# Moving two pieces of matmul work in the head of a gated linear-attention and MLP kernel

## The chip, the cores and the metric

The kernel runs on one core of one Trainium2 chip. The metric is the device time of one execution in microseconds (us). Each kernel also has the profile of one execution. For the kernel before it is a further one; for every later kernel it is the first of the six timed ones, and the other five leave no trace. Its span is about 1.3 us shorter than the device time of that same execution (146.8 against 148.1 us before the change). An execution is marked slow when it is over 1.5% above the fastest of the same kernel, and fast otherwise; only fast ones are compared. The granted clock, the share of TensorE's full clock that the profile reports, was 1.0 in all fast executions.

## The reference, cut to what matters

The kernel computes `g * A(x) + (1 - g) * B(x)` for 2048 tokens of 512 features in bf16. `B` is a two-layer MLP with ReLU (512 to 1376 to 512). `A` is linear attention with 32 heads of 16, whose q and k logits go through a small per-head matrix `w_phi` and a softmax.

```python
pq = einsum("bhsd,hdf->bhsf", q, w_phi);  pk = einsum("bhsd,hdf->bhsf", k, w_phi)
phi_q = concat([softmax(pq), softmax(-pq)]);  phi_k = concat([softmax(pk), softmax(-pk)])
kv = einsum("bhsf,bhsd->bhfd", phi_k, v)          # ... o = (phi_q kv) / den;  a = o @ wo
h  = maximum(x @ w1, 0);  b = h @ w2
return g * a + (1 - g) * b
```

## The kernel before: the parts that the change touches

The kernel is hand-scheduled: each engine has a fixed list of operations, and named events become semaphore waits. TensorE (PE) begins with dummy matmuls, transposes the first 512 tokens of x (`x0`) in three pieces, and then computes the first eight 128-wide units of the MLP's hidden layer for these tokens. Each unit has a PSUM bank of its own, and all eight banks are in use. A "slab" is one 128-row block `t` of W1 applied to the eight units; four slabs add up to the hidden layer. The third piece of x0 (its last quarter, 128 tokens) is transposed into bank 1, the bank that unit 7 needs as well.

```python
# ... loads on SyncE's queue, in this order: x0 pieces 0 and 1, then
loadw1(0, 0, 4 * P, "a")          # W1 row block 0, units 0..3
loadx0(2)                         # last quarter of x0
loadw1(0, 4 * P, 8 * P)           # W1 row block 0, units 4..7
for t in range(1, NDT):
    loadw1(t, 0, 8 * P)           # W1 row blocks 1, 2, 3: 256 KB each
# ... rest of W1, w_phi, WV, then the q and the k weights (transposing loads), then x chunks 1..3

UB = (3, 4, 5, 0, 6, 7, 2, 1)     # bank of each unit
def slab(t, us=range(8), c0=0, c1=512):
    for u in us:                  # one matmul; columns c0:c1 are tokens
        p.op("pe", ... W1[:, t, u*P:(u+1)*P], XT[:, t, c0:c1] ...,
             after=["w10a" if t == 0 and u < 4 else f"w1{t}"]
                   + (free[UB[u]] if c0 == 0 else []) + [XV[h][t] for h in hs], ...)

slab(0, range(4), 0, 384)
for dt in range(4):
    xtr(2, dt, 1, dt * P)         # transpose the last x0 quarter into bank 1
xev("dve", 2, 0, 4, 1)            # VectorE empties bank 1 into XT
slab(0, range(4, 8), 0, 384)      # unit 7 waits for that copy
slab(0, range(8), 384, 512)
for t in range(1, NDT):
    slab(t)
# ... ReLUs, two more units, v tiles 0 and 1
for i in range(4): pre(i)         # q weights times w_phi -> copies pc0..pc3
vtile(2, "dve")
for i in range(4, 8): pre(i)      # k weights times w_phi -> copies pc4..pc7; pc4, pc6 on VectorE
rest(0)                           # 16 small matmuls
# main loop: atile(0) is first
def atile(m):                     # q logits into bank 0, k logits into bank 1
    first = xready(m // 4) + ([f"pc{i}" for i in range(8)] if m == 0 else [])
    order = [(dt, w) for dt in range(NDT) for w in range(2)]    # q and k in turn
    ...
```

The softmax here doesn't subtract the row's maximum and nothing guards it: scores larger than these inputs give would overflow.

## Time and profile before

| | before |
|---|---|
| device time, the three runs at hand before the prediction | 147.78, 147.81, 148.31 us |
| span of the profiled run | 146.8 us |
| TensorE busy | 142.6 us, 97% |
| first slab matmul / first matmul after the four slabs / first atile matmul | 4.73 / 12.36 / 19.59 us |

These lines are from the page of the kernel before: TensorE's busy time, the row of the granted clock in 40 slices, and the chain of work that ended last, by engine.

```profile
PE 142.6 (97%) x969; PEld 73.6 (50%) x986; DVE 92.5 (63%) x157; ACT 72.6 (49%) x125; POOL 52.2 (36%) x62
...
PEclk9999999999999999999999999999999999999999
...
PE 93%; DMA 2%; DVE 2%; issue 1%
```

TensorE is the bound. Next is the view of waits for TensorE: who waited for whom, total us, times, longest.

```profile
PE PS L235 <- DVE ONE L211: 0.4, 1, 0.4
PE PS L332 <- DVE WQK L317: 0.4, 1, 0.4
PE PS L524 <- DVE VS L554: 0.3, 1, 0.3
PE PS L524 <- DMA W<-in_B_w_dram: 0.2, 1, 0.2
```

There are four waits, all in the first 20 us. The change goes for the second and third lines. Next is TensorE's timeline around the first slab (start, duration, what, and in brackets the idle time before it and its releaser).

```profile
3.52 0.95 PE L241 MATMUL PS<-IDN,OT 128*128 128x128 bf16 x7
4.73 0.82 PE L524 MATMUL PS<-XT,W 128*128 128x384 bf16 x4 [0.25 <-DMA W<-in_B_w_dram]
5.39 0.39 PE L241 MATMUL PS<-IDN,OT 128*128 128x128 bf16 x4
5.61 0.65 PE L524 MATMUL PS<-XT,W 128*128 128x384 bf16 x3
6.56 1.00 PE L524 MATMUL PS<-XT,W 128*128 128x384 bf16 x10 [0.30 <-DVE VS L554]
```

The three 384-column matmuls that start at 5.61 us are units 4 to 6; unit 7 comes at 6.56 us. L554 in the bracket is a memset that follows the copy on VectorE: the copy itself is the first of the next lines, which are VectorE's, the second being the two k-weight copies.

```profile
5.81 0.69 DVE L253 CAST XT<-PS 128x512 bf16<-128x512 f32 x1 [1.60 <-PE PS L241]
...
18.33 1.21 DVE L317 CAST WQK<-PS 128x480 bf16<-128x480 f32 x2
```

The x0 copy ends at 6.50 us and unit 7 starts 0.06 us later. The second k-weight copy ends at 19.54 us, and the first atile matmul starts at 19.59 us, as TensorE's timeline there shows:

```profile
18.36 0.86 PE L290 MATMUL PS<-W,XT 128*128 128x97 bf16 x16
19.59 1.59 PE L332 MATMUL PS<-WQK,XT 128*128 128x480 bf16 x7 [0.38 <-DVE WQK L317]
```

The bracket understates such a hole: the profile only models where a matmul ends, and it draws one of 384 columns about 0.33 us long where the next can start 0.163 us after it. The distance between the starts of two matmuls that follow each other without a wait is called a slot here (0.163 us for 384 columns, 0.043 us for the 97 columns of the rest matmuls). The start-to-start loss is the distance between two starts less the slot of the first. The first hole is 6.562 - 5.937 - 0.163 = 0.46 us, and the second 19.595 - 19.008 - 0.043 = 0.54 us. All "losses" below are start-to-start.

The last line of this section is the DMA of W1's second row block, issued at 2.42 us: size, and us from issue to landing.

```profile
W<-in_B_w_dram SPq DMA_DIRECT2D x1, 256.0 KB, 3.7
```

### The profile page before, as it was taken

What the parts mean: (1) busy time and instruction counts of PE and PEld (TensorE: products, weight loads), DVE (VectorE), ACT (ScalarE), POOL (GpSimd) and SP (SyncE); (2) the same over time, 40 slices, a digit from 0 to 9 for tenths busy, and PEclk for the clock granted to TensorE, in tenths of its full rate; (3) what the DMA queues carried; (4) which work ended last, traced back from release to release, by engine and by line L of the source; (5) the groups of instructions that cost most, each with busy time, mean ns of one, the idle gap of its engine ahead of it and who ended that gap; (6) DMA issues with size and microseconds to landing.
All of it is one profiled execution on the core that took longest, in us unless ns stands there. A gap on an engine that the chain in (4) does not pass through costs nothing.

```text
span 146.8 us, 2536 instructions
## 1 busy us (share of the span) xinstructions
PE 142.6 (97%) x969; PEld 73.6 (50%) x986; DVE 92.5 (63%) x157; ACT 72.6 (49%) x125; POOL 52.2 (36%) x62
## 2 busy tenths in 40 slices
PE   8899989999999999999999999999999999999994
PEld 4544654444545544645645555554444444444443
DVE  3427736777688778678698976675444555555342
ACT  3307457887778778877878863022222111111150
POOL 2040001788768678787869820300000000000000
PEclk9999999999999999999999999999999999999999
DMA  5999992038349966335533430454433322322213
GB/s 163 319 266 230 166 234 52 0 71 76 71 80 311 177 196 94 71 71 107 78 71 71 107 71 20 91 108 111 83 82 82 75 71 70 78 71 74 71 43 107
DMA packets 45349, 16.12 MB, mean 110 GB/s; under 512 B 39352, under 2 KB 44824, under 8 KB 45336
## 3 DMA queue, kind: packets, MB, share of 16 engines
q1 hardware_dynamic: 45184, 15.92, 50.0%
q8 instruction: 8, 0.13, 0.4%
q10 hardware_dynamic: 152, 0.03, 0.1%
q14 instruction: 5, 0.04, 0.1%
HBM read 4.41 MB, written 2.10 MB: 44 GB/s over the span
## 4 chain that ended last, share of the span: by engine, by line
PE 93%; DMA 2%; DVE 2%; issue 1%
PE PS L486 25%; PE PS L278 19%; PE PS L332 18%; PE PS L495 9%; PE PS L407 9%; PE PS L524 5%; PE PS L461 3%; PE PS L429 3%; DMA W<-in_B_w_dram 2%; PE PS L290 1%; DVE WQK L509 1%; PE PS L312 1%; DVE XT L253 0%; DVE VS L415 0%; DVE WQK L317 0%
## 5 line engine op out<-in xcount | busy, mean ns | idle before, releaser
L486 PE MATMUL PS<-W,HT 128*128 128x512 bf16 (+3 forms) x182 | 40.2, 366 | 0.3
L375 POOL TENSOR_TENSOR EB<-EB,SC 128x1024 bf16<-128x1024 bf16 x15 | 28.9, 1930 | 25.0 <-DVE SC L373 25.0
L351 ACT ACTIVATE EB<-PS 128x480 bf16<-128x480 f32 (+1 forms) x44 | 30.1, 756 | 14.8 <-PE PS L332 14.8
L500 ACT ACTIVATE TFA<-PS,GT 128x512 bf16<-128x512 f32 x16 | 11.0, 687 | 42.7 <-PE PS L495 36.6
L278 PE MATMUL PS<-XT,W 128*128 128x512 bf16 x124 | 30.2, 379 | 0.2
L332 PE MATMUL PS<-WQK,XT 128*128 128x480 bf16 x128 | 28.5, 366 | 0.4 <-DVE WQK L317 0.4
L371 DVE TENSOR_REDUCE ZB<-EB 128x64 f32<-128x1024 bf16 x15 | 18.3, 1220 | 14.8 <-ACT EB L351 14.8
L509 DVE SCALAR_TENSOR_TENSOR WQK<-PS,OMG,TFA 128x512 bf16<-128x512 f32 (+2 forms) x17 | 12.2, 719 | 23.6 <-ACT TFA L500 22.4
L486 PEld LDWEIGHTS PS<-W,HT 128*128 128x128 bf16 (+1 forms) x187 | 17.0, 98 | 17.4
L264 ACT ACTIVATE HT<-PS 128x512 bf16<-128x512 f32 x35 | 20.3, 614 | 7.7 <-PE PS L524 5.9
L332 PEld LDWEIGHTS PS<-WQK,XT 128*128 128x128 bf16 x128 | 12.5, 98 | 14.1 <-DVE WQK L317 0.5
L278 PEld LDWEIGHTS PS<-XT,W 128*128 128x128 bf16 x128 | 12.0, 98 | 13.2
L386 DVE TENSOR_REDUCE ZB<-EB 128x64 f32<-128x1024 bf16 x16 | 18.6, 1164 | 0.0
L395 POOL TENSOR_TENSOR EB<-EB,SC 128x512 bf16<-128x512 bf16 x16 | 16.9, 1059 | 1.3
L495 PE MATMUL PS<-WO,OT 128*128 128x512 bf16 x62 | 16.0, 378 | 0.1
L407 PE MATMUL PS<-WV,XT 128*128 128x512 bf16 x59 | 15.3, 378 | 0.3
L471 DVE TENSOR_TENSOR WQK<-PS,RDEN 128x512 bf16<-128x512 f32 x16 | 11.1, 692 | 0.6
L495 PEld LDWEIGHTS PS<-WO,OT 128*128 128x128 bf16 x64 | 6.1, 97 | 7.2
L417 ACT ACTIVATE VS<-PS 128x512 bf16<-128x512 f32 x14 | 8.5, 608 | 2.0 <-PE PS L407 2.0
L373 DVE RECIPROCAL SC<-ZB 128x64 f32<-128x64 f32 x16 | 8.8, 553 | 0.5
L407 PEld LDWEIGHTS PS<-WV,XT 128*128 128x128 bf16 x64 | 5.5, 97 | 4.9
L524 PE MATMUL PS<-XT,W 128*128 128x512 bf16 (+2 forms) x39 | 7.4, 336 | 0.6 <-DVE VS L554 0.3
(57 smaller groups left out, 87.5 us busy)
## 6 DMA issues: line engine op xcount, KB each, us to landing
out_dram<-WQK SPq DMA_DIRECT2D x15, 128.0 KB, 1.7
W<-in_B_w_dram SPq DMA_DIRECT2D x2, 640.0 KB, 5.3
W<-in_B_w_dram SPq DMA_DIRECT2D x3, 256.0 KB, 3.9
WV<-in_A_wqkv_dram SPq DMA_DIRECT2D x1, 512.0 KB, 5.8
WO<-in_A_wo_dram SPq DMA_DIRECT2D x2, 256.0 KB, 3.2
W<-in_B_w_dram SPq DMA_DIRECT2D x1, 352.0 KB, 5.3
OT<-in_A_x_dram SPq DMA_DIRECT2D x1, 256.0 KB, 2.8
OT<-in_A_x_dram SPq DMA_DIRECT2D x2, 128.0 KB, 3.1
```

The costliest lines, as they stand in the source:

```text
L264: p.op("act", lambda e: e.activation(dst, src, ACT.Relu), after=[f"h{c}_{kt}"], ev=ev)
L278: p.op("pe", lambda e, t=t: e.matmul(PS[:, bank, :], W1[:, t, kt * P:(kt + 1) * P], XT[:, t, c * 512:(c + 1) * 512], start=(t == 0), stop= ...
L332: p.op("pe", lambda e, dt=dt, which=which: e.matmul(PS[:, which, 0:DE], XT[:, dt, m * P:(m + 1) * P], WQK[:, which, dt * DE:(dt + 1) * DE] ...
L351: p.op("act", lambda e: e.activation(dst, s_, ACT.Exp, scale=scale), after=[f"qk{m}"] + busy, ev=ev)
L371: p.op("dve", lambda e: e.tensor_reduce(zk, ek, AX.X, ALU.add), after=[emk, f"cst{b}"], ev=f"zk{m}")
L375: p.op("pool" if m < NT - 1 else "dve", lambda e: e.tensor_tensor(EB[:, b, 3, :].rearrange("p (g f) -> p g f", f=DH), EB[:, b, 2, :].rearr ...
L386: p.op("dve", lambda e: e.tensor_reduce(ZB[:, b, 0:64].rearrange("p (h s) -> p h s", s=2), bass.AP(tensor=EB, offset=base, ap=[[EBS, P], [ ...
L395: p.op("pool", lambda e: e.tensor_tensor(EB[:, b, 0, :].rearrange("p (h s f) -> p h s f", h=H, s=2)[:, :, 1, :], EB[:, b, 1, :].rearrange( ...
L407: p.op("pe", lambda e, dt=dt: e.matmul(PS[:, bank, :], XT[:, dt, m * P:(m + 1) * P], WV[:, dt, :], start=(dt == 0), stop=(dt == NDT - 1)), ...
L486: p.op("pe", lambda e, kt=kt, M=M: e.matmul(PS[:, bank, 0:n], HT[0:M, kt, m * P:(m + 1) * P], W2[0:M, kt, cs], start=(kt == 0), stop=(kt = ...
L495: p.op("pe", lambda e, t=t: e.matmul(PS[:, bank, :], OT[:, t, m * P:(m + 1) * P], WO[:, t, :], start=(t == 0), stop=(t == NDT - 1)), after ...
L524: p.op("pe", lambda e, u=u: e.matmul(PS[:, UB[u], c0:c1], W1[:, t, u * P:(u + 1) * P], XT[:, t, c0:c1], start=(t == 0 and c0 == 0), stop=( ...
```

## The change

The intent is to give TensorE something to do in both holes. Three units of the second slab are begun while the last x0 quarter is still being emptied, and atile 0 runs its four q matmuls first, which need only the first half of the weight copies.

```diff
 def atile(m):
-            first = xready(m // 4) + ([f"pc{i}" for i in range(8)] if m == 0 else [])
+            first = xready(m // 4)
             ...
+            if m == 0:
+                order = [(dt, w) for w in (0, 1) for dt in range(NDT)]
             ...
-                    after=(first if i == 0 else []) + (free[which] if dt == 0 else []),
+                    after=(first if i == 0 else []) + (free[which] if dt == 0 else [])
+                    + ([f"pc{4 * which + c}" for c in range(4)] if m == 0 and dt == 0 else []),
 # in slab():
-                    ... + (free[UB[u]] if c0 == 0 else [])
+                    ... + (free[UB[u]] if c0 == 0 and t == 0 else [])
 # order of the head:
-        slab(0, range(4, 8), 0, 384)
+        slab(0, range(4, 7), 0, 384)
+        slab(1, range(3), 0, 384)
+        slab(0, (7,), 0, 384)
         slab(0, range(8), 384, 512)
+        slab(1, range(3), 384, 512)
+        slab(1, range(3, 8))
 ...
-        for t in range(1, NDT):
+        for t in range(2, NDT):
             slab(t)
```

Below, "the slab half" is the new order of the head, and "q-first" is the atile half.

More of the change, by code (lines that the diff above doesn't have):

```diff
@@ L526, in slab @@
                     start=(t == 0 and c0 == 0), stop=(t == NDT - 1), skip_group_check=True),
-                    after=["w10a" if t == 0 and u < 4 else f"w1{t}"] + (free[UB[u]] if c0 == 0 else [])
+                    after=["w10a" if t == 0 and u < 4 else f"w1{t}"] + (free[UB[u]] if c0 == 0 and t == 0 else [])
                     + [XV[h][t] for h in hs],
```

## The prediction

> What bounds the kernel. The page gives TensorE 142.6 of 146.8 us (97%), and the chain of work that ended last is 93% TensorE matmuls; the granted clock is full throughout. The table of waits for TensorE shows only four idle stretches, all in the first 20 us: 0.4 us at the very start, 0.25 us for the first piece of W1, 0.30 us in the first slab, 0.38 us ahead of the first atile. No other engine holds TensorE up later. The change goes for the last two stretches. Nothing is removed; only the order changes, so those two holes are the ceiling.
>
> Their true size is from start to start, because the modelled end of a matmul includes its drain. The Trainium skill, "TensorE: Matmul & The Clock Gate", section "Wait — 56ns, not 53.3ns?", gives N / 2.4 GHz + 2.5 ns back to back when warm; the trace agrees (512 columns every 216 ns, 384 every 163, 128 every 56).
> - Hole 1: the last 384-column matmul before it starts at 5.94 us, the next at 6.56 us: 0.625 us for a slot of 0.163, so 0.46 us lost. Unit 7 uses bank 1, which VectorE empties of the last x0 quarter from 5.81 to 6.50 us.
> - Hole 2: the last gate/rest matmul starts at 19.01 us, the first atile matmul at 19.59 us: 0.587 for a slot of 0.043, so 0.54 us lost. It waits for the last of VectorE's two q/k weight copies, pc4 (18.33 to 18.97) and pc6 (18.89 to 19.54).
>
> What the change does.
> (a) Three 384-column matmuls of the second slab (3 x 0.163 = 0.49 us) go into hole 1. They need the second W1 row block. In the trace that DMA is issued at 2.42 us and lands at about 6.15 us (3.7 us from issue to landing), while TensorE would get there at 6.10 us. So I expect a small new wait on that DMA, about 0.1 us, and then no wait for VectorE: the three end their slots at about 6.68 us, after 6.50. Gain 0.36 us (0.1 to 0.46 with the landing).
> (b) With q first, atile 0 needs pc0 to pc3 (done by 17.5) and bank 0, which pc4 frees at 18.97; the rest matmuls end their slots at 19.05, so no wait. Four q matmuls of 0.203 us keep TensorE busy until 19.86 (on the old clock), and pc6 is done at 19.54 us. Hole 2 closes fully: 0.54 us. The 0.36 us shift of (a) moves the copies too, since they follow TensorE, so the two add.
>
> How much stays. Everything later follows TensorE. The x chunks land from 19.07 us and are first used at 22.3; the second q/k weight block lands at 15.43 and is used at 17.5: room for 0.9 us. I expect the sum, 0.90 us, to reach the end.
>
> Predicted time: 147.81 - 0.90 = 146.9 us; 8 times in 10 between 146.5 and 147.4 us (runs before spread over 0.5 us). Chances: faster by over 2% 0.01, within 2% 0.98, slower 0.01.
>
> What would show it: in the waits for TensorE, the VectorE entry of 0.30 us in the slab and of 0.38 us before the atile are gone; instead perhaps one below 0.1 us on the W1 DMA near 6.1 us, at the first second-slab matmul. In the timeline the first atile matmul follows the rest matmuls at one slot's distance, near 18.7 us, and later stages all come 0.9 us earlier.
>
> What would make it wrong: the second W1 block landing later than 6.6 us (then (a) gives nothing); a new wait between the q and k halves on ScalarE's copies (pc5, pc7, done at 19.17); an evacuation or transfer later that was just in time and now holds TensorE; or run-to-run spread as large as the gain.

## The result, and the profile after

| | before | after |
|---|---|---|
| device time, median of 6 runs | 148.05 (147.78 to 148.46) us | 147.51 (147.33 to 147.78) us |
| ratio of fast runs, 95% interval | | 0.9963, 0.9941 to 0.9986 |
| span of the profiled run | 146.8 us | 146.4 us |
| first slab / after the four slabs / first atile | 4.73 / 12.36 / 19.59 us | 4.35 / 12.51 / 19.20 us |

A ratio is the mean time of one kernel's fast runs over the mean of the other's in the same rounds, so it is not quite the ratio of the medians quoted.

The time, 147.51 us, lies 0.11 us above the predicted range, and the gain was 0.54 us where 0.90 us was forecast. Here are the same views of the changed kernel. The page:

```profile
PE 142.3 (97%) x972; PEld 73.2 (50%) x989; DVE 92.4 (63%) x157; ACT 72.5 (50%) x125; POOL 52.1 (36%) x62
...
PEclk9999999999999999999999999999999999999999
...
PE 93%; DMA 3%; SPq 1%; issue 1%; DVE 1%
```

The waits of TensorE:

```profile
PE PS L527 <- DMA W<-in_B_w_dram: 0.8, 3, 0.5
PE PS L235 <- DVE ONE L211: 0.4, 1, 0.4
```

Both VectorE waits of the table before are gone. In their place the wait for pieces of W1 has grown from one of 0.2 us to three with 0.8 us in total. The timeline around the first slab:

```profile
3.83 0.34 PE L241 MATMUL PS<-IDN,OT 128*128 128x128 bf16 x3
4.35 0.82 PE L527 MATMUL PS<-XT,W 128*128 128x384 bf16 x4 [0.19 <-DMA W<-in_B_w_dram]
5.01 0.39 PE L241 MATMUL PS<-IDN,OT 128*128 128x128 bf16 x4
5.56 0.66 PE L527 MATMUL PS<-XT,W 128*128 128x384 bf16 x3 [0.16 <-DMA W<-in_B_w_dram]
6.71 0.82 PE L527 MATMUL PS<-XT,W 128*128 128x384 bf16 x4 [0.48 <-DMA W<-in_B_w_dram]
```

The last line begins with the first second-slab matmul, at 6.71 us. The matmul before it starts at 5.893 us, so 6.705 - 5.893 - 0.163 = 0.65 us are lost, more than the 0.46 us of the hole that was to be filled. Its releaser is the DMA of W1's second row block. Another 0.32 us were lost just before, ahead of unit 4 (5.56 us): the second piece of W1's first row block landed at 5.51 us here, against 5.43 us before, while the matmuls came earlier. That wait is not of the new order, since unit 4 stands at the same place in the old one; but there it would have come out of VectorE's hole, as the trace of r_q_first below shows (0.07 us lost on this piece, then 0.38 us on VectorE).

This is the transfer of the second row block, issued at 2.42 us as before; it now took 4.2 us to land, at 6.66 us instead of 6.15:

```profile
W<-in_B_w_dram SPq DMA_DIRECT2D x1, 256.0 KB, 4.2
```

And TensorE around the first atile:

```profile
18.51 0.86 PE L290 MATMUL PS<-W,XT 128*128 128x97 bf16 x16
19.20 1.78 PE L334 MATMUL PS<-WQK,XT 128*128 128x480 bf16 x8
```

The 16 rest matmuls start at 18.51 us and the first atile matmul 0.69 us later, which is 16 slots of 0.043 us: no hole is left.

The four slabs began 0.37 us earlier in this run, because the first piece of W1 landed earlier (4.31 against 4.68 us), and still ended 0.15 us later (12.51 against 12.36 us). The atile hole of 0.54 us is closed in full. This trace is of the slowest of the six timed executions (147.78 us). From the first atile matmul to the start of the last matmul it is 125.0 us in both traces.

### The profile page after: what moved, and what is told of

The parts are those of the page before. It is cut to its first block, busy times and chain, and to the rows that moved or that the text cites. A ratio compares the mean times of both kernels' runs of the same rounds, so it can differ in the third digit from the quotient of the medians.

```text
span 146.4 us, 2542 instructions
## 1 busy us (share of the span) xinstructions
PE 142.3 (97%) x972; PEld 73.2 (50%) x989; DVE 92.4 (63%) x157; ACT 72.5 (50%) x125; POOL 52.1 (36%) x62
## 4 chain that ended last, share of the span: by engine, by line
PE 93%; DMA 3%; SPq 1%; issue 1%; DVE 1%
PE PS L489 25%; PE PS L278 19%; PE PS L334 18%; PE PS L498 9%; PE PS L410 9%; PE PS L527 4%; DMA W<-in_B_w_dram 3%; PE PS L464 3%; PE PS L432 3%; PE PS L290 2%; PE PS L312 1%; DVE WQK L512 1%; SPq L168 1%; SPq L165 0%
## 5 line engine op out<-in xcount | busy, mean ns | idle before, releaser
L489 PE MATMUL PS<-W,HT 128*128 128x512 bf16 (+4 forms) x183 | 40.1, 366 | 0.2
```

The source lines that it names most:

```text
L489: p.op("pe", lambda e, kt=kt, M=M: e.matmul(PS[:, bank, 0:n], HT[0:M, kt, m * P:(m + 1) * P], W2[0:M, kt, cs], start=(kt == 0), stop=(kt = ...
```

## The experiments

The runs of one call share a chip and the runs of the kernel before. All gave correct results. "Less than before" is the difference of the means of fast executions within one call.

### Each half alone (first call)

Kernel e1_q_first is the kernel before with only the atile part of the diff; e2_slab_only has only the slab part.

> Only the q-first half of the change. Theory (mine now): the hole of 0.54 us ahead of the first atile closes whole and stays closed to the end, so 0.54 us less than before (ratio near 0.9963), as much as the full change gave on the clock; the first slab keeps its start-to-start loss of about 0.46 us on the VectorE copy of the last x0 quarter. Rival A (the prediction's sum): the full change's slab half is worth another 0.36 us, so this run should be about 0.36 us slower than the full change. Rival B (the gain of q-first is partly given back later in the kernel): less than 0.35 us, and some later stretch of matmuls starts less than 0.54 us earlier relative to the first slab.

> Only the slab half of the change. Theory: the three pulled-up matmuls wait for the second row block of W1, whose landing differs from run to run (6.15 us in the trace before, 6.66 in the trace after), so the hole on VectorE turns into one on that DMA: time between 0.3 us less and 0.2 us more than before, mean near 0 (ratio 0.998 to 1.001), and the loss ahead of the first second-slab matmul equals landing plus 0.05 us minus the end of the slot before. Rival A (prediction): 0.36 us less (ratio 0.9976), wait under 0.1 us.

| | mean of 6 | less than before | ratio, 95% |
|---|---|---|---|
| before (11 runs) | 148.35 us | | |
| e1_q_first | 147.63 us | 0.72 us | 0.9953, 0.9923 to 0.9983 |
| e2_slab_only | 147.96 us | 0.39 us | 0.9976, 0.9940 to 1.0011 |

Q-first behaved as the theory said: its trace keeps the VectorE hole (0.46 us) and has no wait ahead of the first atile. The slab half alone did not decide: its mean agrees with the prediction's 0.36 us, just outside the range that I expected, and its interval holds zero. Its trace shows something that I had not expected. The next lines are TensorE's timeline of e2_slab_only around the first slab:

```profile
4.31 1.46 PE L524 MATMUL PS<-XT,W 128*128 128x384 bf16 x4
5.57 0.63 PE L241 MATMUL PS<-IDN,OT 128*128 128x128 bf16 x4
6.00 1.49 PE L524 MATMUL PS<-XT,W 128*128 128x384 bf16 x7
```

The four 384-column matmuls from 4.31 us occupy 1.46 us, against 0.82 us in both traces above. They start every 0.320 us, which is half rate; the last half-rate slot ends at 6.32 us. In the trace before it ended at 4.17 us, in the trace after at 3.31 us. At half rate TensorE came late enough that both the VectorE copy and the second W1 block (landed at 5.84 us) were in time, and there is no hole at all. So what the slab half is worth differs from execution to execution by two things outside the kernel's order: when TensorE reaches full rate, and when a W1 block lands.

### Is it the landing of the second W1 block?

e3_w11_halves is the full change with that block loaded in two halves, so that the pulled-up matmuls need a transfer of 128 KB only:

```diff
-        for t in range(1, NDT):
+        loadw1(1, 0, 4 * P, "a")
+        loadw1(1, 4 * P, 8 * P)
+        for t in range(2, NDT):
             loadw1(t, 0, 8 * P)
```

> The full change, with the second W1 row block loaded as two halves, so that the columns which the three pulled-up matmuls read are a transfer of 128 KB that should land some 0.3 to 0.5 us earlier. Theory: the DMA wait ahead of the first second-slab matmul falls to below 0.15 us and the run is 0.2 to 0.5 us faster than the full change, so 0.75 to 1.0 us less than before (ratio 0.993 to 0.995). Rival (the wait on the DMA is a label only and something else, such as the order of banks or the start of the DMA stream, holds the slab): no faster than the full change, or the loss in the first two slabs stays at 0.5 us or more.

The half landed at 5.29 us, and TensorE's timeline of e3_w11_halves shows the units running on without a break:

```profile
4.32 0.81 PE L529 MATMUL PS<-XT,W 128*128 128x384 bf16 x4
4.96 0.39 PE L243 MATMUL PS<-IDN,OT 128*128 128x128 bf16 x4
5.23 2.34 PE L529 MATMUL PS<-XT,W 128*128 128x384 bf16 x20
```

Its mean was 147.19 us, 1.16 us less than before (ratio 0.9923, 0.9884 to 0.9962), more than the 1.0 us that I expected at most. A repeat gave less:

> The full change with the second W1 row block in halves, beside the full change on one chip. Theory: no wait, or one below 0.15 us, ahead of the first second-slab matmul; 0.1 to 0.5 us faster than the full change, though the third block is then issued 0.47 us later and may cost up to 0.4 us (0.39 us seen). Rival: equal to the full change within 0.1 us.

Here it was 147.50 us on the mean, 0.70 us less than before and equal to the full change beside it (147.49 us), so the expected gain over the full change was missed. Again no wait stood ahead of the second slab (the half landed at 5.70 us), but this trace lost 1.10 us later, on the k weights: see "A third moving part". The halves take the wait away, as the theory said; what this brings in time is not settled (over all three calls with halves, 18 executions, the mean is 147.39 us, standard error 0.13).

The opposite test moves the landing back. e5_after_w11_late is the full change and e6_qfirst_w11_late is q-first alone, both with the second and third W1 blocks issued in swapped order (`for t in (2, 1, 3)`). Beside them ran the full change and q-first.

> The full change again, beside q-first alone on the same chip, for a direct price of the slab half. Theory: what the slab half brings is the VectorE hole (about 0.46 us) less the new wait on the second W1 block, which the landing sets (landings so far 5.84 to 6.66 us against a need near 6.06 us when the matmuls run at full rate early): mean gain over q-first between minus 0.2 and plus 0.3 us, and in its trace the loss ahead of the first second-slab matmul is landing plus 0.05 us minus the end of the slot before. Rival (prediction): 0.36 us faster than q-first alone.

> The q-first half again, on the same chip as the full change. Theory: 0.5 to 0.6 us less than before (ratio 0.996 to 0.9966), no wait ahead of the first atile in its trace, and a loss of 0.1 to 0.46 us in the first slab that VectorE's copy of the last x0 quarter sets. Rival (prediction): 0.36 us slower than the full change.

> The full change with the second and third W1 row blocks issued in swapped order, so that the second lands where the third did (6.8 to 8.0 us in the traces so far, near 7.4). Theory: the first second-slab matmul waits for it one for one, 0.9 to 1.6 us lost there, and the run is 0.5 to 1.0 us slower than the full change. Rival (the landing of that block does not hold the full change): slower by less than 0.2 us.

> The same swap on q-first alone, where the second slab starts only after the whole first one (needed near 6.9 to 7.2 us). Theory: the later landing is mostly covered: 0 to 0.5 us slower than q-first alone, and faster than the full change with the same swap by 0.4 to 0.9 us: the slab half turns from a gain into a loss as the landing moves. Rival: it suffers as much as the full change does, so the two swapped kernels differ by no more than their unswapped ones.

| | mean of 6, or as said | less than before (148.23 us) | ratio, 95% |
|---|---|---|---|
| r_after | 147.53 us | 0.70 us | 0.9952, 0.9926 to 0.9978 |
| r_q_first | 147.35 us | 0.88 us | 0.9941, 0.9918 to 0.9963 |
| e5_after_w11_late (4 fast executions) | 148.68 us | 0.44 us more | 1.0030, 1.0001 to 1.0060 |
| e6_qfirst_w11_late | 148.01 us | 0.23 us | 0.9985, 0.9956 to 1.0014 |

The two slow executions of e5 (151.03 and 150.88 us, granted clock 0.989) are left out; they have no trace, and why they were slow is not known. Q-first did better than I expected here (0.9941 against 0.9960 to 0.9966). The swap cost the full change 1.15 us and q-first 0.66 us; both sizes are above what I expected, and the difference between the two is the point: with the swap the full change is 0.67 us slower than q-first, and without it 0.18 us. In the view of waits of e5_after_w11_late the block stands first:

```profile
PE PS L527 <- DMA W<-in_B_w_dram: 2.1, 1, 2.1
```

There the block landed at 7.88 us and the first second-slab matmul started at 7.925 us. In e6_qfirst_w11_late it landed at 7.37 us, before TensorE came to the second slab, and the trace shows no wait for it:

```profile
PE PS L235 <- DVE ONE L211: 0.4, 1, 0.4
PE PS L527 <- DVE VS L557: 0.3, 1, 0.3
```

So the new slab order puts this landing on the critical path, and the old order covers it. That it counts one for one can be read from the three traces that wait for the whole block at full rate. From the first slab matmul to the landing it is 2.304 us in the trace after, 1.603 us in s_after (below) and 3.565 us in e5; from the first slab matmul to the first one after the four slabs it is 8.158, 7.456 and 9.418 us. The difference is 5.85 us in all three.

In r_after the matmuls ran at half rate until 6.10 us and there was no wait for the block. In r_q_first, full rate from 3.76 us, VectorE's hole was 0.38 us.

### A two by two: slab half or not, block whole or in halves

e10_qfirst_halves is q-first with the same halves as e3.

> The full change, one arm of a two by two on one chip (slab half yes or no, second W1 block whole or in halves). Theory: no faster than q-first alone (difference between minus 0.15 and plus 0.3 us). Rival (prediction): 0.36 us faster than q-first alone.

> Q-first alone, the second arm. Theory: ratio to before 0.994 to 0.9965, and the VectorE hole in the slab visible in its trace unless the matmuls or a W1 block are late.

> The full change with the second W1 block in halves, third arm. Theory: with its data in time the slab half earns what was predicted: 0.2 to 0.5 us faster than q-first with the same halves. Rival A (the slab half never earns, whatever the landing): within 0.15 us of q-first with halves.

> Q-first with the second W1 block in halves, fourth arm. Theory: no faster than q-first with the block whole (between minus 0.1 and plus 0.3 us), since the old slab order does not need the block early, and the later blocks and the q/k weight blocks are issued 0.47 us later. Rival: it gains as the full change does.

| (before: 148.19 us) | block whole | block in halves |
|---|---|---|
| full change | 147.16 us (0.9933, 0.9912 to 0.9953) | 147.49 us (0.9955, 0.9931 to 0.9978) |
| q-first alone | 147.40 us (0.9952, 0.9925 to 0.9979) | 147.64 us (0.9965, 0.9939 to 0.9990) |

Here the full change was 0.24 us faster than q-first, where in the call before it was 0.18 us slower. With halves it was 0.15 us faster, less than the 0.2 to 0.5 us that I expected. Both differences lie outside what I expected, in opposite directions, so within one call neither theory is settled by times. The trace of s_after, though, is the prediction's case: full rate from 4.08 us, the block lands at 6.03 us, the matmul before starts at 5.770 us and the first second-slab matmul at 6.071 us, so 6.071 - 5.770 - 0.163 = 0.14 us is lost. Another 0.11 us is lost just before, on the second piece of the first row block (landed at 5.39 us). The span was 145.8 us. The trace of s_q_first, full rate from 3.08 us, has the VectorE hole at 0.46 us.

### The same hole closed without the early need

e4_split_evac is q-first with the slab order of before, except that the last x0 quarter is transposed after three units instead of four, half into bank 2 and half into bank 1, and emptied by VectorE and ScalarE at once. Two banks are used because of the Trainium skill, "PSUM — Partial Sum Buffer", section "PSUM bank collisions raise a hardware error": two engines may not use one bank in the same partitions at once. No run here tests that.

```diff
-        slab(0, range(4), 0, 384)
+        slab(0, range(3), 0, 384)
         for dt in range(4):
-            xtr(2, dt, 1, dt * P)
-        xev("dve", 2, 0, 4, 1)
-        slab(0, range(4, 8), 0, 384)
+            xtr(2, dt, (2, 1)[dt // 2], dt % 2 * P)
+        xev2()        # VectorE: bank 2, dt 0 and 1 (xv20); ScalarE: bank 1, dt 2 and 3 (xv22)
+        slab(0, range(3, 8), 0, 384)
```

> The q-first half, and the first hole closed another way that needs nothing of the second W1 block earlier than before: the last x0 quarter is transposed after three units in place of four, into two banks, and emptied by VectorE and ScalarE at once (two copies of about 0.42 to 0.5 us in place of one of 0.69). Theory: both holes close, the start-to-start loss in the first slab falls from 0.46 to below 0.1 us without a DMA wait there, time 0.85 to 1.0 us less than before (ratio 0.9935 to 0.994). Rival (the head is bound by the DMA stream in any order): the loss reappears as a wait on the first, second or third piece of W1 or on x0, and the run is no better than q-first alone.

> Both holes closed (q-first and split emptying), beside the full change on one chip. Theory: 0.85 to 1.1 us less than before (ratio 0.9925 to 0.9943) and 0.2 to 0.6 us faster than the full change. Rival: equal to the full change within 0.15 us.

e7_split_only has this edit with q and k in the old order:

> The early, split emptying of the last x0 quarter alone, k and q logits in the old order. Theory: the VectorE hole of the first slab (0.46 us in three of the traces with the old slab order) closes without a new DMA wait, the hole of 0.54 us ahead of the first atile stays: 0.3 to 0.5 us less than before (ratio 0.9966 to 0.998). Rival (the head is bound by the DMA stream, so no order of the first slab gains): ratio 0.999 or more, and the loss returns as a wait on a W1 block.

Beside r_split_evac and e7_split_only ran the full change:

> The full change once more, for comparison on this chip and for a third trace of it. Theory: ratio to before 0.995 to 0.9975; the slab's loss is either a wait on the second W1 block (when the matmuls reach full rate before about 5 us) or a stretch at half rate (when they do not).

And once more on another chip:

> The full change beside the split emptying, a second time on one chip. Theory: 0.6 to 0.9 us less than before; from the first atile matmul to the last matmul 125.0 us, as in all traces so far, so that every difference lies ahead of the first atile.

> Both holes closed without needing the second W1 block early. Theory: 0.9 to 1.1 us less than before and 0.1 to 0.4 us faster than the full change. Rival: equal to the full change within 0.1 us, when the second W1 block comes in time in most executions.

| | mean of 6 | less than before | ratio, 95% |
|---|---|---|---|
| e4_split_evac (first call, with e1) | 147.24 us | 1.11 us | 0.9932, 0.9898 to 0.9966 |
| r_split_evac | 147.18 us | 1.02 us | 0.9931, 0.9902 to 0.9960 |
| e7_split_only (same call) | 147.84 us | 0.37 us | 0.9975, 0.9945 to 1.0005 |
| r2_after (same call) | 147.49 us | 0.71 us | 0.9941, 0.9908 to 0.9974 |
| t_split_evac | 147.32 us | 0.86 us | 0.9941, 0.9911 to 0.9970 |
| t_after (same call) | 147.48 us | 0.71 us | 0.9955, 0.9925 to 0.9984 |

TensorE's timeline of r_split_evac around the first slab:

```profile
4.37 0.78 PE L537 MATMUL PS<-XT,W 128*128 128x384 bf16 x3
5.19 0.40 PE L241 MATMUL PS<-IDN,OT 128*128 128x128 bf16 x4
5.43 2.16 PE L537 MATMUL PS<-XT,W 128*128 128x384 bf16 x16
```

All units run from 5.43 us without a break of 0.1 us, with nothing needed early from the second W1 block. Two sizes lay outside what I expected: e4_split_evac gained 1.11 us where I expected up to 1.0, and t_split_evac 0.86 us where I expected at least 0.9. The split version beat the full change by 0.31 and 0.16 us in the two calls that had both, and has the lowest mean of all orders. Taken together, its 18 timed runs average 147.25 us (standard error 0.07) against 147.44 us (0.05) for 30 runs of the full change: 0.19 us, about twice the combined error. I call it the best of these kernels, by a margin that is small beside the spread of runs. In t_split_evac's trace half rate lasted until 6.38 us, and its span was 146.5 us in spite of the better order.

### A third moving part

The view of waits of r2_after, the full change again, has a line that no earlier trace had:

```profile
PE PS L312 <- DMA PHQ<-in_A_wqkv_dram: 0.8, 1, 0.8
```

The k weights' transposing load landed at 18.22 us there, and at 18.37 us in r_w11_halves, against 15.43 us in the trace before; TensorE wants them at about 16.8 to 17.8 us in most traces. The start-to-start losses were 0.98 and 1.10 us. In e7_split_only it landed at 17.41 us and lost 0.20 us there, which the hole ahead of the atile gave back (0.33 in place of 0.54 us). In the other 17 traces it came in time. This belongs to no half of the change. It goes with one call: in the four traces of the third call (chip 6) this load took 6.21 to 6.93 us from issue to landing, in the other 16 traces 4.75 to 5.13 us. Why is not known, nor whether the executions of that call without a trace had it too. A faster head has less room for such a landing, since the need moves forward.

### What all 20 traces agree on

The distance from the start of the first atile matmul to the start of the last matmul is 125.00 or 125.01 us in all 20 traces, before, after and experiments alike. So nothing after the first atile took part: each difference is made before it. The distance from the first matmul after the slabs to the first atile is 7.23 us in the old order of q and k (before, e2, e7) and 6.69 us with q first, in all traces in which the k weights came in time. Their difference, 0.54 us, is the whole worth of q-first in the traces, whatever the chip.

## Why the prediction was right or wrong

**Right: the bound, and step (b).** TensorE holds the span. Q-first closes the atile hole of 0.54 us in full, and all of it reaches the end: 7.23 against 6.69 us, then 125.0 us unchanged. No wait appeared between the q and k halves on ScalarE's copies.

**Wrong: step (a), "Gain 0.36 us (0.1 to 0.46 with the landing)".** The mechanism was named rightly (the VectorE wait turns into a wait on the second W1 block). The step that failed is the size of that wait, "about 0.1 us": in the trace it was 0.65 us, larger than the hole of 0.46 us, so the term was negative there. The 0.1 us came from one trace, in which the block lands at 6.15 us, 1.42 us after the first slab matmul. With the 5.85 us of the swap experiment that makes 7.27 us for the four slabs, 0.36 us less than the 7.63 us before: the prediction's sum, for that landing. In the trace on record the head began 0.37 us earlier and the block landed 0.51 us later, so the distance was 2.30 us and the slabs took 8.16 us, 0.53 us more than before. In the 14 traces that load this block whole and third, it lands between 5.61 and 6.66 us, or 1.24 to 2.30 us after the first slab matmul; the trace on record has the latest. The range that I gave for (a) had no negative side, though the prediction itself names a landing after 6.6 us as what would spoil it. Q-first's 0.54 us (its worth in the traces) is the whole measured gain of 0.54 us, which leaves about zero for (a).

**Missed: the rate of TensorE in the head.** I took the full rate in the first slab for granted, because the trace before had it from 4.17 us. The last half-rate slot ends anywhere from 3.08 to 6.38 us over the 20 traces. Where it ends late, the matmuls reach the hole late and DMA waits vanish. The slab half is then judged on a different schedule from the one that I costed.

**Wrong: the base.** The prediction starts from 147.81 us, the median of three runs. In the rounds on record the kernel before had 148.05 us, and over all 61 of its runs in this study the mean is 148.22 us (standard error 0.05). With q-first taken at 0.54 us, the miss is therefore the sum of two terms: 0.24 us in the base and 0.36 us in (a), from 146.91 to 147.51 us.

**What stays open.** Over all calls the full change averages 147.44 us (30 runs), 0.78 us less than before, not far from the predicted 0.90. But q-first alone averages 147.46 us (18 runs, standard error 0.07), 0.76 us less than before, although the traces fix its worth at 0.54 us. By pooled means the slab half then adds 0.02 us, with a 95% interval of about 0.18 us either way (twice the combined standard error). The traces say what that mean is made of. Take the time from the first slab matmul to the first matmul after the four slabs, which leaves out when the first W1 block came:

| full rate | old slab order | with the slab half |
|---|---|---|
| by 4.2 us | 7.63 (before), 7.70 (e1), 7.63 (r_q_first), 7.63 (s_q_first) us | 7.46 us (s_after, block at 6.03 us), 8.16 us (after, block at 6.66 us) |
| from 6.0 us on | 8.38 (e6), 8.45 (e10) us, both with other loads | 8.15 (e2), 8.01 (r_after) us |

Two more traces of the full change lie between the rows, with full rate from 5.5 to 5.6 us: 7.76 us both (t_after, r2_after), with no partner in the old order. At late full rate the slab half takes away some 0.2 to 0.4 us. At early full rate, the case that I costed, it takes away 0.17 us with a block near the middle of its landings, and costs 0.53 us with the latest one. It costs when the distance from first slab matmul to landing is above 7.63 - 5.85 = 1.78 us, which is so in only 2 of the 14 traces. An estimate from their mean distance, 1.59 us, is a gain of 0.2 us at early full rate, half of what I predicted. The timed executions other than the profiled ones leave no trace, so how often the block came late in them, and why q-first gained 0.2 us more than its hole, is not known. That late landings use up the slab half's gain on the mean is not shown; that a late landing costs it one for one is shown, by e5 and by the traces after and s_after.

## What to carry to other kernels

Before filling a wait with work pulled forward, look at what that work itself waits for: here it moved a DMA landing from slack onto the critical path, and the landing's spread from run to run (1.05 us) was larger than the hole (0.46 us). In the head of a kernel, size a gain from several traces and not from one, and take the base from as many runs as the gain needs: here three runs misplaced the base by 0.24 us, beside a gain of 0.54 us. A wait can also be shortened at its source (here by splitting a PSUM copy over two engines and starting it one matmul earlier), which needs nothing new from the DMA queue.

## What the Trainium skill lacked or had wrong

- "TensorE: Matmul & The Clock Gate", section "What's actually happening", says that the change to full rate varies by "±500ns"; a note in it adds that the count of matmuls at half rate differs from run to run. Over 20 traces of nearly the same head, with the first matmul at about 0.38 us, the last half-rate slot ended between 3.08 and 6.38 us, a spread of 3.30 us. That is near the 3.4 us window that the same section calls free-running, so "by up to one window" would fit these traces better.
- The same page, section "Wait — 56ns, not 53.3ns?": its slots agree here in both states (128 columns every 106.7 ns at half rate and 56 ns at full rate; 384 columns every 320 and 163 ns; 512 every 216 ns). The same page, section "Seeing it yourself", warns that clock events in a trace have been seen to be unreliable. What it does not say, nor any other page: the profile's row of granted clock shows full in all 40 slices of the traces before and after, while their first slots are at half rate. The rate of the head had to be read from the distances of starts.
- No page gives the spread of one transfer's landing from run to run. The 256 KB block of W1, issued at about 2.42 us in each of 14 traces behind the same transfers, landed at 5.61 to 6.66 us. The k weights' transposing load took 4.75 to 6.93 us from issue to landing over the 20 traces, and the four longest are those of one call.
